# Converting 64-bit weights beside a full TensorE: squares, signs and the identity change engines

## The chip, the cores and the metric

The kernel runs on one core of a Trainium2 chip. The metric is the device time of one execution in microseconds (us). Before the change it is 718.17 us, the median of three runs (717.43 to 720.17). The engines are named as the profile names them: PE is TensorE's matmul and PEld its weight load, DVE is VectorE, ACT is ScalarE, POOL is GpSimd, SP is the queue that issues most transfers.

## The reference

The first part is attention through a small memory, for 8 batches, 8 heads, 576 tokens, head size 64 and 32 memory slots. The second part is a feed-forward layer with 512 inputs and 2048 hidden values:

```python
a = softmax(phi, axis=tokens)                # b h s m
k_m, v_m = a^T k, a^T v                      # b h m d
attn = softmax(q k_m^T / sqrt(64)) v_m       # b h s d
x = attn, heads side by side                 # 4608 x 512
h = x @ w_in
out = (h * cos(h)) @ w_out
```

The two weights `w_in` (512 x 2048) and `w_out` (2048 x 512) come as 64-bit floats; all else is float32.

## The kernel before

**Weights.** [...] Each weight is handled in eight slices of 128 partitions by 1024 numbers: `w_in` in slices of 256 columns (`load_w_in`, `convert_w_in`), `w_out` in slices of 256 rows (`load_w_out`, `convert_w_out`). Three buffers hold raw slices in turn; slices 2 and 3 of `w_in` use space of `w_out` instead. `to_float32` (lines 124 to 142) makes five steps of a slice: the sign goes to the upper half of each float32 (L133, on DVE), the last three bits of the mantissa to the lower half (L135, ACT), the high word is scaled by a power of two (L139, ACT, in place), both are joined by a shift and an or (L140, DVE), and the squares are summed along each partition (L142, ACT, which writes the squares into the raw buffer's low words).

From the sums of squares `weight_scale` (L162 to L174) gets one power of two for each weight: a maximum over the slices (L165, DVE), an all-reduce over the partitions on POOL (L166: `m_in` for `w_in`, `m_out` for `w_out`), and small DVE operations (from L167 on). The power of two brings the weight into the range of two float16 parts. `w_out_split` (L178, L179) and `w_in_split` (L189, L190) make these parts.

**Batches.** `memory(b)` makes the first softmax and `k_m`, `v_m`. For the first four batches the maximum over the tokens is a DVE reduce (L220, `nmx`) and a product with the identity on PE that puts it on all partitions (L223, `top`). It also turns `X` with the identity (L268). An all-reduce on POOL (L288, `l`) gives the batch's power of two (`v_scale`, L152 and L153). `attend(b)` makes the scores (L350) and the second softmax; `fold` multiplies `v_m` into `w_in` (L427, L433), so that one product of depth 256 takes the place of attention's last product and of the first large one.

**Large products.** The 4608 tokens are 12 groups of 384; each has 16 steps `f`, one for 128 of the 2048 hidden values. A step is `gemm1` (the first product), `act` and `act_end` (the cosine, on ACT and DVE) and, four steps later, `gemm2` (the second product). Group 0 works in float32 (L485, L533), as the scales are not known yet, and takes place while the weights arrive; the later groups work with pairs of float16 parts (L494, L538), three passes for one. Values between the two products wait in six `gp` buffers. In each step of group 0 one slice of a weight is converted (`convert_next`), in the order in0, in1 ahead of the steps, then out0, in2, in3, out1, out2, in4, in5, out3, out4, in6, in7, out5, out6, out7. After in7 `weight_scale` runs for `w_in`, after out7 for `w_out`. Group 1 needs both scales.

**Order.** A planner orders each engine's instructions ahead of time by when their inputs should be ready and by their place in the program; some are pinned behind the one before them (`keep_in_program_order`). On the chip each engine runs its list in that order. Two small PSUM banks (`small_ps`, L56) serve all small products in turn. At the start, `warm` issues idle products so that PE does not slow down.

The identity, `ident`, is made on POOL at the start (`make_identity`, a memset and an affine select, which the profile shows as masks.py:197 and masks.py:199).

Of the kernel before, what the change touches and what calls it, by code (L numbers as in the profile page):

```python
# [9 lines left out]

F16 = mybir.dt.float16
F32 = mybir.dt.float32
# [5 lines left out]
AF = mybir.ActivationFunctionType  # L18
ALU = mybir.AluOpType
# [4 lines left out]
P = 128  # L24
# [8 lines left out]
WS = 256  # L33
# [11 lines left out]
@with_exitstack  # L45
def attention_then_ffn(ctx: ExitStack, tc: tile.TileContext, phi, phiT, kv, qT, w_in, w_out, out):
    nc = tc.nc
# [11 lines left out]
    ident = const.tile([P, P], F32, name="ident")  # L59
    make_identity(nc, ident)  # L60
    # in X, heads of even number hold [k | v] and those of odd number [v | k]
    vmask = const.tile([P, 2, 2], F32, name="vmask")
# [4 lines left out]
    w_in_sb = const.tile([P, NP, DF], F32, name="w_in_sb")  # L67
    # w_out: block f + 1 holds rows f * 128 on as float32, later block f their two float16 parts
    wo = const.tile([P, NF + 1, DM], F32, name="wo")
# [30 lines left out]

# [1 line left out]
    raws = itertools.count()  # L102
# [4 lines left out]
    def load_w_in(j):  # L107
        if j in (2, 3):
            # the space of w_out's last blocks, which come later
            t = wo[:, 13:17] if j == 2 else wo[:, 9:13]  # L110
            t = t.bitcast(I32).rearrange("p c (f t) -> p c f t", t=2)
        else:
            t = ld.tile([P, NP, WS, 2], I32, tag=next_raw(), name=f"raw_in_{j}")
        nc.sync.dma_start(out=t, in_=w_in[:, 2 * WS * j:2 * WS * (j + 1)].rearrange("(c p) (f t) -> p c f t", p=P, t=2))
        loads["in", j] = t
# [7 lines left out]

    def to_float32(dst, raw, sq_to, pin=False):
        # the upper half of dst gets the sign, the lower half the last three bits of the mantissa,
        # which lead the low word. The high word as a float32 times 2^-112 has the exponent less
        # 896, three bits too low, and nothing above it.
        low, high = raw[:, :, :, 0], raw[:, :, :, 1]
        flat = raw.rearrange("p c f t -> p c (f t)")
        halves = dst.bitcast(I16).rearrange("p c (f t) -> p c f t", t=2)  # L130
        low_top = flat.bitcast(U8).rearrange("p c (f t) -> p c f t", t=8)[:, :, :, 3]
        high_top = flat.bitcast(I8).rearrange("p c (f t) -> p c f t", t=8)[:, :, :, 7]
        begin = (nc.vector.tensor_scalar(out=halves[:, :, :, 1], in0=high_top, scalar1=0.0, scalar2=-32768.0,  # L133
                                         op0=ALU.is_lt, op1=ALU.mult),
                 nc.scalar.activation(halves[:, :, :, 0], low_top, AF.Copy, scale=2.0 ** -5, bias=-31.0 / 64.0))  # L135
        if pin:
            for ins in begin:
                tc.keep_in_program_order(ins)
        nc.scalar.activation(high.bitcast(F32), high.bitcast(F32), AF.Copy, scale=2.0 ** -112)  # L139
        nc.vector.scalar_tensor_tensor(out=dst.bitcast(I32), in0=high, scalar=3, in1=dst.bitcast(I32),  # L140
                                       op0=ALU.logical_shift_left, op1=ALU.bitwise_or)
        nc.scalar.activation(low.bitcast(F32), dst, AF.Square, accum_out=sq_to)  # L142

    def convert_w_in(j):
        to_float32(w_in_sb[:, :, j * WS:(j + 1) * WS], loads.pop(("in", j)), sq[:, 0, j:j + 1], j == 1)

    def convert_w_out(j):
        to_float32(wo[:, 2 * j + 1:2 * j + 3], loads.pop(("out", j)), sq[:, 1, j:j + 1])

    # e, a power of two, with every magnitude below 2 e; and 2^14 / e  # L150
    def power_of_two(dst, src):
# [10 lines left out]
    def weight_scale(kind, name):  # L162
        # halving the exponent of the largest sum of squares
        m = const.tile([P, 1], F32, name=f"m_{name}")
        nc.vector.tensor_reduce(out=m, in_=sq[:, kind], op=ALU.max, axis=AX.X)  # L165
        nc.gpsimd.partition_all_reduce(m, m, channels=P, reduce_op=RED.max)  # L166
        nc.vector.tensor_scalar(out=m, in0=m, scalar1=2.0, scalar2=2.0 ** -100, op0=ALU.mult, op1=ALU.max)  # L167
        nc.vector.tensor_scalar(out=m.bitcast(I32), in0=m.bitcast(I32), scalar1=1, scalar2=None,
                                op0=ALU.logical_shift_right)
        nc.vector.tensor_scalar(out=m, in0=m, scalar1=2.0 ** 63, scalar2=None, op0=ALU.mult)  # L170
        e = const.tile([P, 1], F32, name=f"e_{name}")
        power_of_two(e, m)
        st["e", name] = e
        st["s", name] = to_range(f"s_{name}", const, f"s_{name}", e)  # L174
# [6 lines left out]

    # w_in in two float16 parts. A head's 64 rows of both parts are brought together on the 128
    # partitions, so that one pass takes both: the first part stays where it is, the second goes to
    # the other half. The slices are kept where a load or an earlier slice was.
    def w_in_split(q, c):
# [17 lines left out]

    # the maximum over the tokens, on all partitions, far ahead of its use
    def maximum(b):
# [7 lines left out]

# [1 line left out]
    def memory(b):  # L215
        a = loads.pop(("phi", b))
        if b < NT:
            # by the tensor engine, from phi transposed
            nmx = wk.tile([P, 2], F32, tag="nmx", name=f"nmx_{b}", bufs=1)
            nc.vector.tensor_reduce(out=nmx, in_=loads.pop(("phiT", b)), op=ALU.max, axis=AX.X)  # L220
            top = small_ps(f"top_{b}")[:, 0:HM]
            for g in range(2):
                nc.tensor.matmul(top[:, g * P:(g + 1) * P], lhsT=nmx[:, g:g + 1].broadcast_to([P, P]), rhs=ident,  # L223
                                 start=True, stop=True)
        else:
            top = st["top", b]
# [4 lines left out]
        for c0, c1, n in ((0, 2, P), (2, 4, P), (4, 5, S - 512)) if b == 0 else ((0, 4, P), (4, 5, S - 512)):  # L231
            ins = nc.vector.tensor_tensor(out=a[:n, c0:c1], in0=a[:n, c0:c1],
                                          in1=top[:n].unsqueeze(1).broadcast_to([n, c1 - c0, HM]),
                                          op=ALU.subtract)
            if b >= NT:
                # not sooner: the maximum takes its time
                tc.keep_in_program_order(ins)
            nc.scalar.activation(a[:n, c0:c1], a[:n, c0:c1], AF.Exp)  # L238
# [53 lines left out]

    # the powers of two that bring the two-part float16 operands into range
    def v_scale(b):
# [4 lines left out]
    def scales(b):  # L299
# [10 lines left out]
        else:  # L310
            # the first part of v_m for both parts of w_in, the second part for the first one alone
            sv = to_range(f"sv_{b}", wk, "sv", st["ev", b])
# [9 lines left out]

    # attention over the memory: scores with (head, memory) on the partitions; 32 by 32 blocks are
    # transposed for the softmax over a head's memory, and back
    def attend(b):
        qt, km = loads.pop(("q", b)), st["km", b]
        flat = wk.tile([P, 4 * S], F16, tag="aT", name=f"aT_{b}", bufs=3)
        # the first group works in float32, on the first GT tokens of the first batch
        t32 = GT if b == 0 else 0
# [90 lines left out]

    # v_m folded into w_in
    def fold_psum(b, q, g):
# [46 lines left out]

# [1 line left out]
    def regions(grp):  # L471
# [53 lines left out]
    def gemm2(grp, f, gp):  # L525
        if f == 0:
            # nothing else is left for the small tiles' banks beside the last group
            spare = 2 if grp == 11 else 0
# [11 lines left out]
        if f == NF - 1:  # L540
            # the last group waits for the third accumulator of the one before alone
            for t in (2,) if grp == 10 else range(3):
                evacuate(grp, t)
# [24 lines left out]

# [1 line left out]
    load_phi(0)  # L570
# [31 lines left out]
    fold_first(1)  # L602
    # the other weights, in the order in which they are needed, each a step of the first group
    todo = [("out", 0)]
# [48 lines left out]
    for i in range(12 * NF):  # L653
# [16 lines left out]
        begun.append((grp, f, hp, *act(grp, f, hp, last)))  # L670
        # with nothing else between them, a step's first half goes before the second half of the one before
        while len(begun) > (grp >= 9):
# [31 lines left out]

_INS = ["phi", "phiT", "kv", "qT", "w_in", "w_out"]

# [32 lines left out]
```

## Time and profile before

| what | value |
| --- | --- |
| median of three runs | 718.17 us |
| the profiled execution: span | 718.0 us |
| PE busy | 694.5 us |
| DVE busy | 569.6 us |
| ACT busy | 520.3 us |
| POOL busy | 14.6 us |
| mean granted clock of PE | 0.993 |
| sums of squares (L142): 16 | mean 1.16 us each, without the accumulator's read |
| signs (L133): 16 | 0.71 to 0.77 us each |
| conversions, first to last | 22 to 110 us |

The span runs from the first to the last instruction. The page of the profile gives the busy time of each engine, the chain of waits, and the costliest groups of instructions by line; the timeline lists instructions in order of time, with the idle time ahead of them and who ended it in brackets. Matmuls are pipelined and their ends are modelled, so a busy PE is not of itself one at its full pace; starts that follow each other tell more.

### The profile page before, as it was taken

How to read it: one execution, taken by the hardware profiler on the slowest of the kernel's cores; microseconds unless marked ns; L12 is line 12 of the kernel's file. 1: busy time of each engine (PE TensorE's matmuls, PEld its weight loads, DVE VectorE, ACT ScalarE, POOL GpSimd, SP SyncE). 2: the span in 40 equal slices, each digit the busy share in tenths (PEclk: the TensorE clock that was granted, in tenths of full speed). 3: DMA queues.
4: the chain of work that ended last, by engine and by line, in shares of the span. 5: the costliest groups of instructions: out<-in, count | busy, mean ns of one | idle time of the engine just before them, and what ended most of it. 6: DMA issues, size and time to landing. Idle time of an engine off the chain costs nothing.

```text
span 718.0 us, 12024 instructions
## 1 busy us (share of the span) xinstructions
PE 694.5 (97%) x4578; PEld 357.3 (50%) x4578; DVE 569.6 (79%) x1257; ACT 520.3 (72%) x964; POOL 14.6 (2%) x36
## 2 busy tenths in 40 slices
PE   6689999999999999999999999999999999999997
PEld 2345444565454444565444444566444544555553
DVE  2779999998988997589877897669776987676763
ACT  1699999889886875678756685668767785665553
POOL 0000000000000000000000100000000000000000
PEclk9799999999999999999999999999999999999999
DMA  9994981526405300152104310152100000100101
GB/s 282 382 326 159 310 306 30 132 60 188 148 8 160 110 1 1 45 166 67 45 1 135 96 48 1 45 168 67 44 1 1 22 25 1 45 1 1 45 0 45
DMA packets 31417, 66.72 MB, mean 93 GB/s; under 512 B 2176, under 2 KB 10880, under 8 KB 31360
## 3 DMA queue, kind: packets, MB, share of 16 engines
q1 hardware_dynamic: 27040, 58.09, 25.5%
q10 hardware_dynamic: 4320, 7.87, 2.9%
q8 instruction: 36, 0.59, 0.3%
q14 instruction: 21, 0.17, 0.1%
HBM read 52.31 MB, written 9.44 MB: 86 GB/s over the span
## 4 chain that ended last, share of the span: by engine, by line
PE 59%; DVE 20%; ACT 14%; issue 3%; DMA 3%; POOL 0%; SPq 0%; DVEq 0%; ACTq 0%; POOLq 0%
PE acc L538 34%; PE hp L494 18%; PE pv L433 3%; DVE u L517 3%; DVE gp L520 2%; DVE u L509 2%; DMA phi<-in_phi 2%; ACT u L513 2%; DVE gp L508 2%; ACT L513 1%; DVE vw L440 1%; PE psA L248 1%; ACT raw_out L142 1%; DVE wo L179 1%; PE sc L350 1%
## 5 line engine op out<-in xcount | busy, mean ns | idle before, releaser
L538 PE MATMUL acc<-wo,gp 128*128 128x512 f16 x1584 | 371.3, 379 | 0.0
L538 PEld LDWEIGHTS <-gp 128*128 128x128 f16 x1584 | 153.4, 98 | 161.6 <-issue 2.6
L494 PE MATMUL hp<-aT,vw 128*128 128x192 f16 (+1 forms) x1440 | 202.9, 284 | 1.4 <-DVE u L517 1.2
L494 PEld LDWEIGHTS <-vw 128*128 128x128 f16 x1440 | 125.0, 98 | 84.0 <-issue 30.7
L513 ACT ACTIVATE u<-u 128x384 f32<-128x384 f32 x192 | 99.9, 524 | 88.5 <-DVE u L509 87.4
L517 DVE SCALAR_TENSOR_TENSOR u<-hp,u 128x384 f32<-128x384 f32 x176 | 96.9, 553 | 45.8 <-ACT u L513 43.5
L503 ACT ACTIVATE u<-hp,cu 128x192 f32<-128x192 f32 (+1 forms) x240 | 110.9, 492 | 17.0 <-PE hp L494 10.8
L520 DVE TENSOR_TENSOR gp<-u,gp 128x384 f16<-128x384 f32 x176 | 96.6, 552 | 29.8 <-ACT gp L519 29.3
L519 ACT CAST gp<-u 128x384 f16<-128x384 f32 x176 | 89.2, 509 | 40.0 <-DVE u L517 37.9
L509 DVE TENSOR_TENSOR u<-u,gp 128x384 f32<-128x384 f32 x192 | 105.8, 552 | 3.1
L508 DVE CAST gp<-u 128x384 int32<-128x384 f32 x192 | 67.4, 354 | 20.4 <-ACT u L503 18.7
L533 PE MATMUL acc<-wo,gp 128*128 128x512 f32 x96 | 45.5, 599 | 0.2 <-DVE gp L515 0.2
L440 DVE SCALAR_TENSOR_TENSOR vw<-pv,vw 128x512 f16<-128x512 f32 x48 | 33.1, 689 | 4.7 <-ACT vw L439 3.4
L439 ACT ACTIVATE vw<-pv 128x512 f16<-128x512 f32 x48 | 28.3, 591 | 6.4 <-PE pv L433 5.5
L485 PE MATMUL hp<-aT,vf 128*128 128x384 f32 x64 | 26.4, 545 | 4.2 <-DVE gp L515 2.0
L513 ACT ACT_TABLE_LOAD x23 | 29.5, 1283 | 0.4
L533 PEld LDWEIGHTS acc<-wo,gp 128*128 128x128 f32 x96 | 17.2, 190 | 17.4 <-issue 12.9
L248 PE MATMUL psA<-kv,phi 128*32 128x129 f32 (+1 forms) x640 | 23.5, 277 | 0.8 <-ACT phi L238 0.8
L554 ACT ACTIVATE ob<-acc,os 128x512 f32<-128x512 f32 x28 | 18.5, 683 | 8.0 <-PE acc L538 6.1
L248 PEld LDWEIGHTS psA<-kv,phi 128*32 128x32 f32 (+1 forms) x640 | 16.0, 109 | 11.2 <-issue 5.9
L485 PEld LDWEIGHTS hp<-aT,vf 128*128 128x128 f32 x64 | 12.4, 206 | 17.2 <-issue 5.3
L350 PE MATMUL sc<-q,km 128*64 128x256 f32 (+3 forms) x192 | 20.2, 336 | 0.0
(129 smaller groups left out, 553.3 us busy)
## 6 DMA issues: line engine op xcount, KB each, us to landing
kv<-in_kv SPq DMA_DIRECT2D x32, 516.0 KB, 5.8
q<-in_qT SPq DMA_DIRECT2D x8, 1152.0 KB, 5.7
raw_out<-in_w_out SPq DMA_DIRECT2D x8, 1024.0 KB, 5.5
out<-ob ACTq DMA_DIRECT2D x30, 256.0 KB, 2.1
raw_in<-in_w_in SPq DMA_DIRECT2D x6, 1024.0 KB, 7.3
phi<-in_phi SPq DMA_DIRECT2D x8, 512.0 KB, 6.7
w_in_sb<-w_in_parts SPq DMA_DIRECT2D x12, 256.0 KB, 4.6
phiT<-in_phiT SPq DMA_DIRECT2D x4, 576.0 KB, 8.0
```

The lines of the kernel that those rows point to most:

```text
L248: nc.tensor.matmul(psA[32 * j:32 * (j + 1), g * KV:(g + 1) * KV], lhsT=a[:n, c, h * M:(h + 1) * M], rhs=kvs[c][:n, h * KV:(h + 1) * KV], s ...
L440: nc.vector.scalar_tensor_tensor(out=vw[:, 1, g], in0=src, scalar=T, in1=vw[:, 0, g], op0=ALU.mult, op1=ALU.subtract)
L494: nc.tensor.matmul(hp[:, c0:c0 + n], lhsT=vw[:, wi, g, fo * P:(fo + 1) * P], rhs=aT[:, ai, g, c1:c1 + n], start=(k == 0), stop=(k == 5))
L503: ins = nc.scalar.activation(u[:, c0:c0 + n], hp[:, c0:c0 + n], AF.Copy, scale=st["cu", b] if grp else 1.0 / (2.0 * math.pi), bias=0.25)
L508: nc.vector.tensor_copy(out=ni, in_=u)
L509: nc.vector.tensor_tensor(out=u, in0=u, in1=ni, op=ALU.subtract)
L513: nc.scalar.activation(u, u, AF.Sin, scale=TWO_PI_BELOW)
L517: nc.vector.scalar_tensor_tensor(out=u, in0=hp[:, :GT], scalar=2.0 ** -17, in1=u, op0=ALU.mult, op1=ALU.mult)
L519: nc.scalar.copy(gp[:, 0], u)
L520: nc.vector.tensor_tensor(out=gp[:, 1], in0=u, in1=gp[:, 0], op=ALU.subtract)
L533: nc.tensor.matmul(accs[grp][t], lhsT=gp[:, t * P:(t + 1) * P], rhs=wo[:, f + 1], start=(f == 0), stop=(f == NF - 1))
L538: nc.tensor.matmul(accs[grp][t], lhsT=gp[:, gi, t * P:(t + 1) * P], rhs=parts[:, wi], start=(f == 0 and gi == 0 and wi == 0), stop=(f == N ...
```

## The change

The identity becomes an input, `eye`, which the first transfer on SP's queue brings. In `to_float32` the sign's engine becomes an argument: DVE for slices 0 to 2 of `w_in`, POOL for the other five and for all eight of `w_out`. The sum of squares no longer runs on ACT. In its place PE takes the upper halves of the finished float32 numbers as bf16 (every second halfword), multiplies each of eight blocks of 128 columns with itself, and adds the eight products in one small PSUM bank; on the diagonal stand sums of squares. DVE takes the maximum of each row. The raw buffer is no longer written after L140. Where this text speaks of Gram products, it means these.

```diff
     ident = const.tile([P, P], F32, name="ident")
-    make_identity(nc, ident)
+    nc.sync.dma_start(out=ident, in_=eye)
...
-    def to_float32(dst, raw, sq_to, pin=False):
+    def to_float32(dst, raw, sq_to, by, pin=False):
...
-        begin = (nc.vector.tensor_scalar(out=halves[:, :, :, 1], in0=high_top, scalar1=0.0, scalar2=-32768.0,
-                                         op0=ALU.is_lt, op1=ALU.mult),
+        begin = (by.tensor_scalar(out=halves[:, :, :, 1], in0=high_top, scalar1=0.0, scalar2=-32768.0,
+                                  op0=ALU.is_lt, op1=ALU.mult),
...
-        nc.scalar.activation(low.bitcast(F32), dst, AF.Square, accum_out=sq_to)
+        tops = dst.bitcast(BF16).rearrange("p c (f t) -> p c f t", t=2)
+        gram = small_ps("gram")[:, 0:P]
+        cols = [tops[:, c, x:x + P, 1] for c in range(dst.shape[1]) for x in range(0, dst.shape[2], P)]
+        for i, w in enumerate(cols):
+            nc.tensor.matmul(gram, lhsT=w, rhs=w, start=(i == 0), stop=(i == len(cols) - 1))
+        nc.vector.tensor_reduce(out=sq_to, in_=gram, op=ALU.max, axis=AX.X)
 
     def convert_w_in(j):
-        to_float32(w_in_sb[:, :, j * WS:(j + 1) * WS], loads.pop(("in", j)), sq[:, 0, j:j + 1], j == 1)
+        to_float32(w_in_sb[:, :, j * WS:(j + 1) * WS], loads.pop(("in", j)), sq[:, 0, j:j + 1],
+                   nc.vector if j < 3 else nc.gpsimd, j == 1)
 
     def convert_w_out(j):
-        to_float32(wo[:, 2 * j + 1:2 * j + 3], loads.pop(("out", j)), sq[:, 1, j:j + 1])
+        to_float32(wo[:, 2 * j + 1:2 * j + 3], loads.pop(("out", j)), sq[:, 1, j:j + 1], nc.gpsimd)
```

More of the change, by code (lines that the diff above doesn't have):

```diff
@@ L7 @@
 from concourse import bass_isa, mybir
-from concourse.masks import make_identity
 from concourse._compat import with_exitstack
+BF16 = mybir.dt.bfloat16
 F16 = mybir.dt.float16
@@ L45, in attention_then_ffn @@
 @with_exitstack
-def attention_then_ffn(ctx: ExitStack, tc: tile.TileContext, phi, phiT, kv, qT, w_in, w_out, out):
+def attention_then_ffn(ctx: ExitStack, tc: tile.TileContext, phi, phiT, kv, qT, w_in, w_out, eye, out):
     nc = tc.nc
@@ L702, in attention_then_ffn @@
         gemm2(*p)
-_INS = ["phi", "phiT", "kv", "qT", "w_in", "w_out"]
+_INS = ["phi", "phiT", "kv", "qT", "w_in", "w_out", "eye"]
 def kernel(**inputs):
@@ L725 @@
         "w_out": np.ascontiguousarray(w_out).view(np.int64),
+        "eye": np.eye(P, dtype=np.float32),
     }
```

## The prediction

> **What bounds the kernel now.** I read the page's span first, then the busy time by stage, then the timeline of PE, then the start and GpSimd's queue.
>
> ```profile
> span 718.0 us, 12024 instructions
> ```
>
> ```profile
> 0.00:46.00 46.00, 30.13 (x180) 14.38 (x182) 23.86 (x49) 22.63 (x29) 1.84 (x10) 0.89 0.99 331
> 46.00:112.00 66.00, 65.47 (x308) 31.36 (x305) 62.86 (x136) 65.78 (x100) 1.94 (x6) 1.00 0.72 249
> ```
>
> The second fence gives, for a stage, the busy time of PE, PEld, DVE, ACT and POOL, then the granted clock, the DMA share and GB/s. The profiled execution took 718.0 us and the median of the three times is 718.17, so I sum against 718. All conversions of weights lie before 112 us. From 46 to 112 us PE, DVE and ACT are all busy 95% or more, and a busy PE need not be a full one. The timeline of PE settles it:
>
> ```profile
> 61.85 0.61 PE L268 MATMUL tpx<-ident,X 128*128 128x128 f32 x4
> 62.30 1.02 PE L533 MATMUL acc<-wo,gp 128*128 128x512 f32 x2
> 63.16 0.49 PE L485 MATMUL hp<-aT,vf 128*128 128x384 f32 x1
> ```
>
> Two float32 passes of 512 columns give way to the next after 0.86 us (63.16 less 62.30), four of 128 after 0.45 us: 0.84 and 0.88 ns a column. Long and short ones run at one pace, so it is the columns that take the time and no pauses hide in the busy share. After 46 us, then, two things alone change the time: work that PE gains or loses, and inputs so late that PE stops. Before 46 us PE idles for 15.9 us, and a faster start pays one for one.
>
> **Start: the identity by DMA.** First from the chain of waits, then the timeline, then the DMA issues with their us to landing:
>
> ```profile
> 0.87 0.32 POOL km L271
> ...
> 1.24 0.01 POOLq masks.py:199
> 1.25 9.56 issue
> ```
>
> ```profile
> 4.65 1.35 DVE L220 TENSOR_REDUCE nmx<-phiT 128x2 f32<-128x1152 f32 x1 [2.96 <-DMA phiT<-in_phiT]
> 5.12 0.59 SPq L98 DMA_DIRECT2D q<-in_qT  x1
> 6.05 3.90 SPq L114 DMA_DIRECT2D raw_in<-in_w_in  x2
> 11.14 1.22 PE L223 MATMUL top<-ident,nmx 128*128 128x128 f32 x4 [4.94 <-POOL ident masks.py:199]
> 22.08 1.37 ACT L135 ACTIVATE w_in_sb<-raw_in 128x1024 int16<-128x1024 uint8 x1
> 22.42 1.52 PE L350 MATMUL sc<-q,km 128*64 128x256 f32 x16
> 26.27 1.12 ACT L139 ACTIVATE raw_in<-raw_in 128x1024 f32<-128x1024 f32 x1 [2.81 <-DVE w_in_sb L133]
> 27.42 1.23 DVE L140 SCALAR_TENSOR_TENSOR w_in_sb<-raw_in,w_in_sb 128x1024 int32<-128x1024 int32 x1 [0.36 <-ACT raw_in L139]
> ```
>
> ```profile
> q<-in_qT SPq DMA_DIRECT2D x1, 1152.0 KB, 13.2
> raw_in<-in_w_in SPq DMA_DIRECT2D x1, 1024.0 KB, 15.0
> ```
>
> The first maximum `top` has its `nmx` at 6.0 and starts at 11.14, for the identity. One more issue at the head of SP's queue pushes the others by some 0.5 us (an issue's own time), so `top` could start at 6.5, 4.6 us sooner. Other inputs end most of this. The batch's q lands at 18.3 (5.12 + 13.2); after the same push the scores can start 3.6 us sooner than 22.42. The first raw slice lands at 21.05 (6.05 + 15.0), and the chain L135, L139, L140 of 3.72 us then ends at 25.3 and not at 28.65, 3.4 us sooner. I take 3.1, between bounds of 0.5 (what L135 itself can move) and 4.6.
>
> **ScalarE loses the squares.** A row of the groups by line, and two of the waits:
>
> ```profile
> L142 ACT ACTIVATE raw_out<-wo 128x1024 f32<-128x1024 f32 x8 | 9.3, 1165 | 0.1
> ```
>
> ```profile
> PE hp L485 <- DVE gp L515: 2.0, 1, 2.0
> ...
> PE hp L485 <- ACT vf L458: 0.7, 1, 0.7
> ```
>
> Sixteen times 1.165 us is 18.6 us of ACT. After 46 us that is no gain by itself, as PE is full. Before, it is worth what PE waits for in its first steps behind ACT's queue, 2.0 + 0.7 us. I take 2.0, bounds 0 and 2.7. The raw buffers also come free a square earlier, so SP can issue the next raw loads sooner.
>
> **TensorE gains the Gram products:** eight matmuls of 128 by 128 bf16 for each of 16 slices, each with its own weight load. No row has this form. The float32 passes above give 0.112 us for 128 columns (0.45 by four), an upper bound. The timeline gives a lower one; the groups by line have what VectorE needs:
>
> ```profile
> 114.81 1.15 PE L494 MATMUL hp<-aT,vw 128*128 128x192 f16 x12
> 115.81 1.05 PE L533 MATMUL acc<-wo,gp 128*128 128x512 f32 x2
> ```
>
> ```profile
> L133 DVE TENSOR_SCALAR wo<-raw_out 128x1024 int16<-128x1024 int8 x8 | 6.0, 755 | 0.0
> ...
> L282 DVE TENSOR_REDUCE l<-X 128x4 f32<-128x256 f32 x2 | 0.8, 411 | 0.0
> ```
>
> Twelve f16 products of 192 columns give way after 1.00 us, 83 ns each, with a weight load of the same size hidden; by columns, 128 would be 56 ns. I take 70, between that and the 83, which is the nearest row. Thirteen of the 16 slices fall into the full stretch: 104 x 70 ns = 7.3 us, bounds 5.8 and 11.6. The other three fall into idle time. Their banks come from the two small ones and are freed by VectorE's maximum. That reduce is some 0.25 us (half the elements of the row of 0.41): 16 x 0.25 = 4.0 us more for DVE, against 13 signs less, 13 x 0.755 = 9.8. DVE gains 5.8 us, which the full PE hides.
>
> If nothing else happened: 718.0 - 3.1 - 2.0 + 7.3 = 720.2.
>
> **GpSimd gains 13 signs.** This decides. From GpSimd's timeline:
>
> ```profile
> 0.73 0.20 POOL masks.py:197 MEMSET ident<- 128x128 f32 x1 [0.29 <-POOLq L727]
> ...
> 10.80 0.28 POOL masks.py:199 TENSOR_SCALAR_AFFINE_SELECT ident<-ident 128x128 f32<-128x128 f32 x1 [9.62 <-issue]
> ...
> 21.40 0.38 POOL L288 PARTITION_ALL_REDUCE l<-l  x1 [9.79 <-DVE l L286]
> ...
> 66.59 0.37 POOL L288 PARTITION_ALL_REDUCE l<-l  x1 [19.37 <-DVE l L286]
> ...
> 96.09 0.35 POOL L166 PARTITION_ALL_REDUCE m_in<-m_in  x1 [18.32 <-DVE m_in L165]
> ...
> 110.42 0.35 POOL L166 PARTITION_ALL_REDUCE m_out<-m_out  x1 [13.73 <-DVE m_out L165]
> ...
> 231.56 1.09 POOL L211 PARTITION_ALL_REDUCE mx<-mx  x1 [4.31 <-DVE mx L210]
> ```
>
> The price of one: memsets of 128 and 256 elements take 0.20 and 0.32 us, 0.9 ns an element more, so 0.95 us for 1024 is the lower end. The affine select's 0.28 for 128 would make 2.3 us, the all-reduce's 1.09 for 256 would make 4.4. The sign is a comparison and a multiplication on bytes eight apart, into halfwords four apart; I take 4.4, nearest to the all-reduce as work of several steps for each element.
>
> The affine select stood 9.56 us behind a mark of the queue, with nothing shown that released it. Memsets have no such gap, and the first all-reduce comes after 9.8 idle us, in which one could hide. I read the gap as code being fetched for another kind of instruction. The sign is another kind than the all-reduce, and the new queue mixes them: the all-reduces of l_0 and l_1 (line 288), m_in and m_out (line 166) lie among the signs. I take 9.56 us for each change of kind.
>
> The Trainium skill, GPSIMD Engine Reference, section 2.1, has such libraries of loadable code, and gives the first call after a load some 6 us. The 9.56 us here agree in kind and are longer; by its figure each change below would cost 3.6 us less.
>
> The queue, worked out on the old times: l_0 comes at 18, the first change ends at 28, and seven signs (out0, in3, out1, out2, in4, in5, out3) fit before l_1, which I put at 65 (66.6 less 5.1 from the start, and six slices' products more). Then two changes and the all-reduce, 65 + 19.1 + 0.4 = 84.5. The signs of out4, in6 and in7 last until 97.7. Now m_in could start at 100.4 (L140, products and reduces: 2.7), but out5's sign runs until 102.1; with its change m_in starts at 111.7 and not 96.1. Change back, 121.6; out6 and out7 until 130.4; their tail of 2.7 and the last change: m_out at 142.7, not 110.4.
>
> ```profile
> 114.85 0.75 DVE L179 SCALAR_TENSOR_TENSOR wo<-wo,s_out 128x512 f16<-128x512 f32 x1
> ...
> 127.10 0.81 PE L538 MATMUL acc<-wo,gp 128*128 128x512 f16 x3
> ```
>
> From m_out to the first split block of w_out are 5.2 us (110.42 to 115.60), so the first f16 product, now at 127.1, comes at 147.9, 20.8 us later. Meanwhile PE can go one step of first products ahead (six `gp` buffers, five in use): the 1.00 us of above. The Gram products and the start's gain then lie inside PE's wait. All engines execute in order: behind L152 and L167, which wait for an all-reduce, stands the rest of DVE's work, and behind a Gram product of a late slice all of PE's. **Forecast: 718.0 + 20.8 - 1.0 = 737.8, say 738.** Bounds: with signs at 0.95 us the same queue has m_out before 125, which hides it all, and leaves the 720 of above. If the earlier stops, at out4's slice and at m_in, are not made good, each may add what a change costs, some 10 us.
>
> **Rivals.**
>
> *GpSimd locks VectorE.* From the timeline of both:
>
> ```profile
> 562.07 0.56 DVE L520 TENSOR_TENSOR gp<-u,gp 128x384 f16<-128x384 f32 x1
> 562.19 0.65 POOL L288 PARTITION_ALL_REDUCE l<-l  x1 [69.40 <-DVE l L286]
> ```
>
> This all-reduce takes 0.65 us, not 0.35, beside a DVE operation with two operands in SBUF, and ends after it. If DVE in turn waits for whole signs, then 11 signs after 46 us at half of 4.4 us each are 24 us, on a DVE with 3.1 idle and 5.8 freed: 15 us on top, 753. Against it: no row has DVE waiting. Chance 0.15. The Trainium skill, SBUF — State Buffer, section on SBUF's two separate sides, has an exclusive lock in both directions; the row agrees for the one.
>
> *No change of kind is paid*, or an order hides it. Then the sum above holds, 720.2. Thirteen signs of 4.4 us are 57 of the 84 us from 28 to 112. For it: one gap alone is seen for sure. Chance 0.16.
>
> *Faster: the start decides.* GpSimd keeps up as in the last, and the full stretch begins much sooner: by 4.6 from the identity, 2.7 from the squares, and 2.3 because the first steps of group 0 no longer run at a slow pace after an idle PE:
>
> ```profile
> 32.20 5.46 PE L485 MATMUL hp<-aT,vf 128*128 128x384 f32 x8 [1.43 <-DVE aT L373]
> ...
> 43.24 1.56 PE L485 MATMUL hp<-aT,vf 128*128 128x384 f32 x4 [1.98 <-DVE gp L515]
> ```
>
> Eight took 5.46 us, and twice four later ones would take 3.12. With products at 56 ns: 718.0 - 9.6 + 5.8 = 714.2. It is faster from 9.4 us gained at the start on. Against it: DMA is busy 0.99 of that stage, and sets when the slices come. Chance 0.13.
>
> **How the numbers follow.** Forecast 0.56, lock 0.15, nothing paid 0.16, faster 0.13. A measurement can tell about 0.5% here, 3.6 us. Faster: 0.13. Same: the most of the 720 case and the lower edge of the forecast, 0.17. Slower: 0.70. The range reaches from 713, under the faster case, to 762, the lock with part of the 10 us; the forecast's own range is 722 to 750.
>
> **What would show it.** Right: gaps near 9.6 us on POOL before all-reduces and before signs that follow them, signs near 4.4 us, m_out near 143, and over 15 us of idle PE between 75 and 150 us. The start is right if `top` begins near 6.5 and the first L485 near 29. Wrong: POOL without such gaps, or PE full from 46 us on; then the time is near 720, or less if the full stretch begins by 37.

## The result, and the profile after

The changed kernel takes 758.37 us (median of four runs, 756.71 to 760.93), against 718.75 for the kernel before on the same chip: a ratio of 1.0541 [1.0509, 1.0572]. It is slower by twice what was forecast. The profiled execution took 757.45 us. Line numbers of the changed kernel are 7 or 8 higher from `weight_scale` on: the first product of group 0 is L493 (L485 before), that of the later groups L502 (L494), the second products L541 and L546 (L533 and L538).

The page of the changed kernel, its span, its busy times and its clock:

```profile
span 755.6 us, 12282 instructions
...
PE 709.2 (94%) x4706; PEld 368.8 (49%) x4706; DVE 573.0 (76%) x1259; ACT 507.0 (67%) x933; POOL 68.6 (9%) x47
...
PEclk9679899799999999999999999999999999999999
```

Busy time by stage, the kernel before and then the changed one (PE, PEld, DVE, ACT, POOL, granted clock, DMA share, GB/s; the first two stages of the kernel before stand in the prediction):

```profile
112.00:170.00 58.00, 57.26 (x365) 31.77 (x363) 57.83 (x118) 53.36 (x110) 0.31 (x1) 1.00 0.33 79
```

```profile
0.00:46.00 46.00, 23.35 (x158) 11.25 (x158) 21.70 (x44) 16.30 (x18) 10.34 (x10) 0.76 0.91 319
46.00:112.00 66.00, 55.98 (x340) 30.32 (x340) 48.63 (x95) 47.74 (x62) 34.19 (x11) 0.91 0.71 242
112.00:170.00 58.00, 49.68 (x201) 24.18 (x200) 39.67 (x96) 36.12 (x63) 13.23 (x6) 0.90 0.16 51
```

All is lost before 170 us. In those 170 us PE is busy for 129.01 us instead of 152.86, and a part of that at half clock; what follows is 585.6 us of span instead of 548.0. The 46 us at the start, where the forecast saw a gain, lose 6.8 us of PE's work.

GpSimd's timeline in the changed kernel (start, duration, instruction, idle time ahead and what ended it):

```profile
17.30 0.35 POOL L296 PARTITION_ALL_REDUCE l<-l  x1 [15.76 <-DVE l L294]
26.72 4.04 POOL L133 TENSOR_SCALAR wo<-raw_out 128x1024 int16<-128x1024 int8 x1 [9.07 <-DMA raw_out<-in_w_out]
32.12 4.94 POOL L133 TENSOR_SCALAR w_in_sb<-wo 128x1024 int16<-128x1024 int8 x1 [1.36 <-DMA wo<-in_w_in]
52.33 0.31 POOL L279 MEMSET km<- 128x256 f32 x1 [15.27 <-PE sc L358]
52.61 7.98 POOL L133 TENSOR_SCALAR wo<-raw_out 128x1024 int16<-128x1024 int8 x2
...
87.53 0.43 POOL L296 PARTITION_ALL_REDUCE l<-l  x1 [5.96 <-issue]
97.51 4.05 POOL L133 TENSOR_SCALAR wo<-raw_out 128x1024 int16<-128x1024 int8 x1 [9.55 <-ACT u L511]
...
116.10 0.38 POOL L174 PARTITION_ALL_REDUCE m_in<-m_in  x1 [6.29 <-issue]
...
123.47 11.84 POOL L133 TENSOR_SCALAR wo<-raw_out 128x1024 int16<-128x1024 int8 x3 [6.74 <-issue]
143.91 0.76 POOL L174 PARTITION_ALL_REDUCE m_out<-m_out  x1 [8.60 <-DVE m_out L173]
```

A sign takes 4.0 to 5.1 us, and before each change between signs and all-reduces GpSimd stands still for 6 to 9.6 us. `m_out` comes at 143.9; the forecast had 142.7. One idle stretch was not foreseen: the memset of `km` at 52.33 waits 15.27 us for the scores of batch 0 on PE, and two signs stand behind it.

PE at the start of the changed kernel:

```profile
16.76 0.61 PE L276 MATMUL tpx<-ident,X 128*128 128x128 f32 x4
24.97 1.03 PE L148 MATMUL gram<-w_in_sb 128*128 128x128 bf16 x8 [7.61 <-DVE w_in_sb L140]
25.81 2.33 PE L590 MATMUL warm<-zeros 128*128 128x512 f16 x5
28.07 2.83 PE L358 MATMUL sc<-q,km 128*64 128x256 f32 x16
43.29 2.90 PE L493 MATMUL hp<-aT,vf 128*128 128x384 f32 x4 [11.25 <-DVE aT L381]
```

The Gram products of the first slice stand ahead of the scores in PE's order. They wait 7.61 us for the slice, and the scores wait with them. The first product of group 0 comes at 43.29, not near 29.

PE at the end of the conversions, from the timeline and from the windows of the changed kernel:

```profile
129.94 1.03 PE L148 MATMUL gram<-wo 128*128 128x128 bf16 x8 [4.35 <-DVE wo L140]
...
137.95 1.01 PE L148 MATMUL gram<-wo 128*128 128x128 bf16 x8 [3.97 <-DVE sq L149]
...
144.21 1.98 PE L541 MATMUL acc<-wo,gp 128*128 128x512 f32 x4
...
...
168.61 1.67 PE L546 MATMUL acc<-wo,gp 128*128 128x512 f16 x7
```

```profile
120.00:142.00 22.00, 13.68 (x43) 6.20 (x42) 8.52 (x14) 11.36 (x17) 11.84 (x3) 0.80 0.00 0
142.00:170.00 28.00, 28.00 (x130) 13.90 (x128) 26.14 (x58) 21.21 (x41) 0.76 (x1) 0.97 0.23 66
```

The first f16 second product comes at 168.61, 24.7 us after `m_out` and not 5.2. PE isn't waiting for the split in those 24.7 us: it is full from 142 us on, with float32 products of group 0 that it could not do while the slices were late. The first split block of `w_out` is ready at 150.59 us (L187, at 149.85 for 0.74 us), 18 us before PE comes to it.

### The profile page after: what moved, and what is told of

Same layout as the page of the kernel before. It is cut to its first block, busy times and chain, and to the rows that moved or that the text cites. A ratio compares the mean times of both kernels' runs of the same rounds, so it can differ in the third digit from the quotient of the medians.

```text
span 755.6 us, 12282 instructions
## 1 busy us (share of the span) xinstructions
PE 709.2 (94%) x4706; PEld 368.8 (49%) x4706; DVE 573.0 (76%) x1259; ACT 507.0 (67%) x933; POOL 68.6 (9%) x47
## 4 chain that ended last, share of the span: by engine, by line
PE 66%; DVE 13%; ACT 7%; POOL 5%; DMA 4%; issue 3%; SPq 1%; ACTq 0%; POOLq 0%; DVEq 0%
PE acc L546 37%; PE hp L502 19%; POOL wo L133 4%; PE pv L441 3%; DMA raw_out<-in_w_out 3%; DVE u L517 2%; PE psA L256 2%; DMA phi<-in_phi 2%; DVE u L525 1%; PE sc L358 1%; DVE gp L528 1%; DVE gp L516 1%; DVE wo L187 1%; POOL w_in_sb L133 1%; DVE vw L448 1%
## 5 line engine op out<-in xcount | busy, mean ns | idle before, releaser
L546 PE MATMUL acc<-wo,gp 128*128 128x512 f16 x1584 | 370.7, 379 | 0.0
L546 PEld LDWEIGHTS <-gp 128*128 128x128 f16 x1584 | 153.6, 98 | 161.3 <-issue 1.8
L502 PE MATMUL hp<-aT,vw 128*128 128x192 f16 (+1 forms) x1440 | 202.1, 284 | 0.4 <-DVE u L525 0.3
L502 PEld LDWEIGHTS <-vw 128*128 128x128 f16 x1440 | 125.0, 98 | 80.7 <-issue 28.0
L511 ACT ACTIVATE u<-hp,cu 128x192 f32<-128x192 f32 (+1 forms) x240 | 110.5, 490 | 19.9 <-PE hp L502 14.0
L517 DVE TENSOR_TENSOR u<-u,gp 128x384 f32<-128x384 f32 x192 | 108.3, 565 | 3.4
L541 PE MATMUL acc<-wo,gp 128*128 128x512 f32 x96 | 48.3, 630 | 0.0
L493 PE MATMUL hp<-aT,vf 128*128 128x384 f32 x64 | 28.8, 573 | 13.6 <-DVE aT L381 11.2
L133 POOL TENSOR_SCALAR wo<-raw_out 128x1024 int16<-128x1024 int8 x8 | 33.0, 4146 | 32.0 <-DMA raw_out<-in_w_out 15.7
L296 POOL PARTITION_ALL_REDUCE l<-l x8 | 4.0, 504 | 333.5 <-DVE l L294 327.6
L541 PEld LDWEIGHTS acc<-wo,gp 128*128 128x128 f32 x96 | 18.2, 199 | 18.2 <-issue 15.4
L493 PEld LDWEIGHTS hp<-aT,vf 128*128 128x128 f32 x64 | 13.1, 220 | 26.3 <-issue 18.5
```

The lines of the kernel that those rows point to most:

```text
L133: begin = (by.tensor_scalar(out=halves[:, :, :, 1], in0=high_top, scalar1=0.0, scalar2=-32768.0, op0=ALU.is_lt, op1=ALU.mult), nc.scalar.a ...
L493: nc.tensor.matmul(hp[:, :GT], lhsT=st["vf", q][:, g, fo * P:(fo + 1) * P], rhs=st["aTf"][:, g], start=(g == 0), stop=(g == 1))
L502: nc.tensor.matmul(hp[:, c0:c0 + n], lhsT=vw[:, wi, g, fo * P:(fo + 1) * P], rhs=aT[:, ai, g, c1:c1 + n], start=(k == 0), stop=(k == 5))
L511: ins = nc.scalar.activation(u[:, c0:c0 + n], hp[:, c0:c0 + n], AF.Copy, scale=st["cu", b] if grp else 1.0 / (2.0 * math.pi), bias=0.25)
L517: nc.vector.tensor_tensor(out=u, in0=u, in1=ni, op=ALU.subtract)
L541: nc.tensor.matmul(accs[grp][t], lhsT=gp[:, t * P:(t + 1) * P], rhs=wo[:, f + 1], start=(f == 0), stop=(f == NF - 1))
```

## The experiments

The theory after the result: two losses of nearly equal size. GpSimd's queue delays the slices by about the forecast's term, and beside it the first slice's Gram products hold up PE's queue at the start, which the forecast had at nothing. The rivals: the lock between GpSimd and VectorE; the length of the signs alone; the Gram products' own work. To compare kernels timed beside different runs of the kernel before, "+x us" below is (ratio − 1) times 720 us, about the median of the kernel before throughout. The changed kernel is then +39.0.

**One part undone.** All signs back on VectorE, the rest of the change as it is:

```diff
-                   nc.vector if j < 3 else nc.gpsimd, j == 1)
+                   nc.vector, j == 1)
...
-        to_float32(wo[:, 2 * j + 1:2 * j + 3], loads.pop(("out", j)), sq[:, 1, j:j + 1], nc.gpsimd)
+        to_float32(wo[:, 2 * j + 1:2 * j + 3], loads.pop(("out", j)), sq[:, 1, j:j + 1], nc.vector)
```

> The changed kernel, but all 16 signs stay on VectorE. Queue theory (GpSimd's signs and its changes of kind make the slices and both scales late): most of the loss goes, 715 to 727 us, with Gram products and the identity's transfer still in. Gram theory (the products on PE, their work and their place in PE's order, make the loss): 745 us or more. Start theory (the loss is made before 46 us by the new order at the start): the first product of group 0 (L493) still near 43 us, and the time near 729.

Measured: 730.63 us, 1.0148 [1.0117, 1.0178], +10.7. The windows of this kernel:

```profile
0.00:46.00 46.00, 23.04 (x168) 11.36 (x170) 23.47 (x48) 16.58 (x19) 1.36 (x8) 0.81 0.93 320
46.00:112.00 66.00, 65.53 (x396) 34.90 (x393) 60.79 (x139) 60.14 (x80) 2.60 (x5) 1.00 0.75 258
```

Without signs on GpSimd, PE is full from 46 us on, as before the change. So the signs make all the stops after 46 us, 28 us of the loss. But the start stays as slow as in the changed kernel (23.04 us of PE's work, 23.35 there, 30.13 before; the first product at 41.63 us): GpSimd's signs have no part in that. This is what the start theory expected: a late first product, and a time near 729.

The squares back on ScalarE, the rest as it is:

```diff
-        tops = dst.bitcast(BF16).rearrange("p c (f t) -> p c f t", t=2)
...
-        nc.vector.tensor_reduce(out=sq_to, in_=gram, op=ALU.max, axis=AX.X)
+        nc.scalar.activation(low.bitcast(F32), dst, AF.Square, accum_out=sq_to)
```

> The changed kernel, but the squares are summed on ScalarE again; signs on GpSimd and the identity's transfer stay. Queue theory: the changes of kind stay, m_out stays near 140 us, and the time is 735 to 755. Gram theory: 722 us or less. If PE is held mainly because Gram products of late slices stand ahead of other work in its order, the time lies between, near 735.

Measured: 737.65 us, 1.0256 [1.0229, 1.0284], +18.4. From its PE timeline, and from its GpSimd timeline:

```profile
18.77 1.52 PE L353 MATMUL sc<-q,km 128*64 128x256 f32 x16
...
28.56 4.43 PE L488 MATMUL hp<-aT,vf 128*128 128x384 f32 x8 [1.43 <-DVE aT L376]
...
74.10 1.98 PE L459 MATMUL pvf<-w_in_sb,vm 128*64 128x256 f32 x8 [4.62 <-DVE w_in_sb L140]
...
82.50 1.98 PE L459 MATMUL pvf<-w_in_sb,vm 128*64 128x256 f32 x8 [4.72 <-DVE vf L461]
...
143.12 0.81 PE L541 MATMUL acc<-wo,gp 128*128 128x512 f16 x3 [0.76 <-ACT ob L553]
```

```profile
59.38 1.26 POOL L291 PARTITION_ALL_REDUCE l<-l  x1 [5.99 <-issue]
67.52 7.92 POOL L133 TENSOR_SCALAR w_in_sb<-raw_in 128x1024 int16<-128x1024 int8 x2 [6.88 <-issue]
...
135.23 0.38 POOL L169 PARTITION_ALL_REDUCE m_out<-m_out  x1 [5.89 <-DVE u L512]
```

The start is now as forecast: scores at 18.77, first product at 28.56. What is left is GpSimd's queue, and it alone costs what the forecast gave for the whole. But PE does not stand still where the forecast put it, behind `m_out`. It idles for 4.8 us from 46 to 75 us and for 8.6 us from 75 to 120 us (where the granted clock is 0.84). The two longest stops are shown: 4.62 us for a slice of `w_in` whose sign came at 67.52, behind the all-reduce `l` and two changes of kind, and 4.72 us for a copy, `vf`, that stands behind two more late slices in VectorE's order. From 120 to 143 us PE idles for 1.1 us. The first split block of `w_out` is ready at 141.84 us, and PE is busy with earlier products until 142.35. The stops at and after 143.12, 3.0 us in all, end with group 0's results being copied out (`ob`), in part by a VectorE that is busy for 8.9 of the 9 us from 143 to 152.

It follows that the sums of squares on TensorE cost 20.6 us in the changed kernel.

**One part alone.** The kernel before with the identity by DMA, and nothing else of the change:

```diff
-    make_identity(nc, ident)
+    nc.sync.dma_start(out=ident, in_=eye)
```

> The kernel before, with nothing changed but the identity, which comes by DMA. By the prediction's term the start gains 3.1 us: 715. Start theory (the earlier identity makes the planner choose a worse order on PE and VectorE): slower, up to 729.

Measured: 720.09 us over ten runs, 1.0002 [0.9989, 1.0015], +0.1. The first product starts 1.2 us sooner (30.98), but the product with the first slice waits longer (`pvf L456`, 5.8 us in the waits, 5.1 before) and later stops give the rest back (`acc L533` waits 1.6 us for VectorE, 0.2 before).

The kernel before with the Gram block in place of the square:

```diff
-        nc.scalar.activation(low.bitcast(F32), dst, AF.Square, accum_out=sq_to)
+        tops = dst.bitcast(BF16).rearrange("p c (f t) -> p c f t", t=2)
...
+            nc.tensor.matmul(gram, lhsT=w, rhs=w, start=(i == 0), stop=(i == len(cols) - 1))
+        nc.vector.tensor_reduce(out=sq_to, in_=gram, op=ALU.max, axis=AX.X)
```

> The kernel before, with nothing changed but the squares, which become Gram products on PE. By the prediction's terms 7.3 us more on PE and 2.0 less at the start: 723. Gram theory: 740 or more. If ScalarE's relief were worth more than the products cost: under 716.

Measured: 733.72 us, 1.0197 [1.0175, 1.0219], +14.2. Its PE timeline:

```profile
26.44 1.03 PE L147 MATMUL gram<-w_in_sb 128*128 128x128 bf16 x8 [4.45 <-DVE w_in_sb L141]
27.28 2.33 PE L588 MATMUL warm<-zeros 128*128 128x512 f16 x5
29.54 2.73 PE L356 MATMUL sc<-q,km 128*64 128x256 f32 x16
...
43.96 2.26 PE L491 MATMUL hp<-aT,vf 128*128 128x384 f32 x3 [10.45 <-DVE aT L379]
```

The time lies between the readings. The picture is that of the changed kernel, without any sign on GpSimd: products, warm products, scores, and the first product of group 0 at 43.96.

The kernel before with 13 signs on GpSimd, the identity still made there (the diff is the one of the change, for `by` alone):

```diff
-        begin = (nc.vector.tensor_scalar(out=halves[:, :, :, 1], in0=high_top, scalar1=0.0, scalar2=-32768.0,
+        begin = (by.tensor_scalar(out=halves[:, :, :, 1], in0=high_top, scalar1=0.0, scalar2=-32768.0,
```

> The kernel before, with nothing changed but the 13 signs, which go to GpSimd; the identity is made there too, so one more change of kind comes at the start. Queue theory: slower by 15 to 45 us, 735 to 760, with gaps of 6 to 10 us at each change of kind. Gram theory: within 5 us of before.

Measured: 740.86 us, 1.0289 [1.0261, 1.0318], +20.8. Here `m_out` comes at 140.52 and the first f16 second product at 148.44, 7.9 us after it, as with the squares on ScalarE (135.23 and 143.12). Again PE does not wait for `m_out`: it idles for 12.2 us from 75 to 120 us and for 0.6 us from 120 to 143 us.

**What makes up the signs' price.** The changed kernel with the four early all-reduces (`l_0`, `l_1`, `m_in`, `m_out`) replaced by a product with the identity and a maximum, so that GpSimd runs nothing but signs and memsets while weights arrive:

```diff
+    def all_max(dst, src, name):
+        t = small_ps(name)[:, 0:P]
+        nc.tensor.matmul(t, lhsT=src.broadcast_to([P, P]), rhs=ident, start=True, stop=True)
+        nc.vector.tensor_reduce(out=dst, in_=t, op=ALU.max, axis=AX.X)
...
-        nc.gpsimd.partition_all_reduce(m, m, channels=P, reduce_op=RED.max)
+        all_max(m, m, f"all_{name}")
```

> The changed kernel, but the four small all-reduces of the first stage (l_0, l_1, m_in, m_out) are made by a product with the identity on PE and a maximum on VectorE, so that no change of kind lies among the signs, which stay on GpSimd. If the changes of kind make the loss: 718 to 730 us, with signs back to back. If the length of the signs (4 us and not 0.75) makes it: 740 or more.

Measured: 743.63 us, 1.0332 [1.0308, 1.0355], +23.9. Some of GpSimd's timeline:

```profile
52.92 8.00 POOL L133 TENSOR_SCALAR wo<-raw_out 128x1024 int16<-128x1024 int8 x2
...
76.65 9.48 POOL L133 TENSOR_SCALAR wo<-raw_out 128x1024 int16<-128x1024 int8 x2 [7.27 <-DMA raw_out<-in_w_out]
...
111.41 5.07 POOL L133 TENSOR_SCALAR wo<-raw_out 128x1024 int16<-128x1024 int8 x1 [1.01 <-DMA raw_out<-in_w_out]
```

With one kind of instruction left, no sign has an idle gap ahead of it that nothing ends: each waits for a transfer or not at all. The last sign ends at 116.5 instead of 135.3. The changes of kind thus cost 15.1 us of the 39.0 in this kernel. Most of the loss stays, as the second reading has it; beside the signs' length the Gram products are still in it.

The changed kernel with the sign of `w_out`'s first slice on VectorE:

```diff
-        to_float32(wo[:, 2 * j + 1:2 * j + 3], loads.pop(("out", j)), sq[:, 1, j:j + 1], nc.gpsimd)
+        to_float32(wo[:, 2 * j + 1:2 * j + 3], loads.pop(("out", j)), sq[:, 1, j:j + 1], nc.gpsimd if j else nc.vector)
```

> The changed kernel, but the sign of w_out's first slice stays on VectorE. If VectorE's wait for this one sign (behind which the first softmax stands in its order) makes the late start: the first product of group 0 (L493) comes near 36 us and not at 43, and the time falls by 5 to 8 us. If the Gram products of the first slice, which stand ahead of the scores in PE's order, make it: L493 moves by 2 us at most.

Measured: 759.29 us over three executions (a fourth, of 3223 us, is left out, and with it the only trace), 1.0533 [1.0489, 1.0577], +38.4. The time is that of the changed kernel, so this sign on GpSimd is not what costs it. Where the first product of group 0 starts here is not on record.

The kernel before with the identity by DMA and the maxima on PE, so that no change of kind stands in GpSimd's queue while weights arrive (the two diffs above together):

> The kernel before, with the identity by DMA and the four small all-reduces of the first stage made on PE and VectorE; nothing else changed. No code is fetched by GpSimd ahead of 180 us. If GpSimd's part in the start is only the identity: as with the identity alone, within 2 us. A candidate for a kernel better than both: 713 or less.

Measured: 717.49 us over ten runs, 0.9971 [0.9948, 0.9995], −2.1. Measured again:

> The same kernel as e8, in five rounds, since its gain was at the edge: 0.3% faster than before, interval below 1. If the start's 2.7 us are given back to inputs that come later: no more than 2 us faster.

Measured: 718.5 us over twelve runs, 0.9985 [0.9969, 1.0001], −1.1. At most 0.3% faster than the kernel before, and not certainly that: beside the identity alone, which makes no difference, it is the only version here that is not slower.

**Where the Gram products stand.** The changed kernel, with the first slice's Gram products issued after the scores and the first fold; nothing else of the program is changed, though the planner then orders every engine anew:

```diff
+        if later:
+            st["late"] = dst, sq_to
+            return
+        squares(dst, sq_to)
...
+    squares(*st.pop("late"))
```

> The changed kernel, but the Gram products of w_in's first slice are issued behind the scores and the first fold and not ahead of them. If their place in PE's order makes the late start: the scores start near 19 us and not at 28, the first product of group 0 (L499 here) near 30 and not at 43, and the time falls by 5 to 6 us, to about 752. If VectorE's order makes it (rival): L499 stays after 40.

Measured: 745.09 us, 1.0357 [1.0337, 1.0378], +25.7. Its PE timeline:

```profile
18.55 1.52 PE L364 MATMUL sc<-q,km 128*64 128x256 f32 x16
25.36 1.98 PE L470 MATMUL pvf<-w_in_sb,vm 128*64 128x256 f32 x8 [5.29 <-DVE w_in_sb L140]
27.27 1.03 PE L154 MATMUL gram<-w_in_sb 128*128 128x128 bf16 x8
28.76 5.33 PE L499 MATMUL hp<-aT,vf 128*128 128x384 f32 x8 [0.46 <-DVE aT L387]
```

Eight matmuls in another place make the kernel 13.3 us faster. That is over twice what I expected, and not all of it is their place on PE: GpSimd's second all-reduce `l` now comes at 59.80 us and not at 87.53, ahead of three signs that it stood behind. The same move in the kernel before with the Gram products:

> The kernel before with Gram products alone (733.7), those of the first slice again behind the scores. Place theory: the start is that of the kernel before, and what is left of the loss is PE's own work, 6.5 us: 725 to 728. Rival (the products cost more than their streaming throughout): 731 or more.

Measured: 721.98 us, 1.0038 [1.0021, 1.0055], +2.7, where the Gram block without the move had +14.2. I had expected 725 to 728. So the place costs 11.5 us of the 14.2, here without signs on GpSimd. What is left, the products' work less ScalarE's relief, is 2.7.

Last, the signs on GpSimd with none of the rest in their way: identity by DMA, squares on ScalarE, maxima on PE (diffs above):

> Signs on GpSimd and the identity by DMA, squares on ScalarE, the four small all-reduces on PE and VectorE: no change of kind among the signs and no Gram products. If the parts add (changes of kind 15, Gram products 14 to 21): 722 to 726. If the signs' length alone still stops PE as long as in e6: 735 or more.

Measured: 725.2 us, 1.0084 [1.0062, 1.0106], +6.0, within the 722 to 726 of the first reading. That is 8.1 us more than the same kernel without the signs (−2.1; 7.1 by its second measurement): what signs on GpSimd cost by their length and their place in its queue, without any change of kind.

## Why the prediction was wrong

The sign of the result was right, and so was GpSimd's queue as one cause, with about its size. The size of the whole was 20 us short, for a term that stood at nothing. And the wait of PE that the forecast put behind `m_out` lies elsewhere.

**GpSimd's queue: right in cause, near in size.** The forecast's 20.8 us less 1.0 stand against +18.4 (signs with the start in order) and +20.8 (signs alone). A sign was put at 4.4 us and took 4.0 to 5.1. A change of kind was put at 9.56 and took between 5.96 and 9.55; the Trainium skill, GPSIMD Engine Reference, section 2.1, gives some 6 us, which the shorter gaps agree with and the longer ones don't. `m_in` was put at 111.7 and came at 116.1, `m_out` at 142.7 and 143.9. Part of that agreement is luck: the second `l` came at 87.53 and not at 65, out5's sign came after `m_in` and not before it, the changes were shorter, and the wait behind the memset of `km` was not in the sum. That the changes are paid at all is shown by replacing the all-reduces (+39.0 to +23.9), so the rival "no change of kind is paid" falls. That code is fetched in these gaps stays a reading: the trace shows idle time alone.

**The step that failed** is "The other three fall into idle time", with its sequel "The Gram products and the start's gain then lie inside PE's wait". The three early slices' products were priced by their length, and their place in PE's order wasn't asked for. All the Gram products together cost 20.6 us in the changed kernel (+39.0 against +18.4), 13.3 of them by the place of the first slice's. There the first slice's products stand behind `tpx` and ahead of five warm products and the scores. The scores' inputs are there from about 18.4 us on (with the products moved, the scores run at 18.55), but they start at 28.07: 7.61 us of waiting for the slice, 0.84 for the products, 2.3 for the warm ones. Two things make 9.5 us into 14.5 at the first product of group 0 (43.29 against 28.76). The scores run at half clock after the wait (granted 0.50 from 24.97 to 30.90 us), 2.83 us and not 1.52. And the first softmax on VectorE and ScalarE now meets the conversions of the next slices. VectorE's timeline in the changed kernel, from the scores on:

```profile
30.09 1.30 DVE L360 STREAM_TRANSPOSE at<-sc 128x512 f32<-128x512 f32 x2 [3.76 <-PE sc L358]
31.97 1.23 DVE L140 SCALAR_TENSOR_TENSOR wo<-raw_out,wo 128x1024 int32<-128x1024 int32 x1 [0.57 <-ACT raw_out L139]
...
34.66 0.94 DVE L365 TENSOR_TENSOR at<-at,rm 128x768 f32<-128x768 f32 x1
35.95 1.22 DVE L140 SCALAR_TENSOR_TENSOR w_in_sb<-wo,w_in_sb 128x1024 int32<-128x1024 int32 x1 [0.35 <-ACT wo L139]
...
40.05 1.22 DVE L140 SCALAR_TENSOR_TENSOR w_in_sb<-wo,w_in_sb 128x1024 int32<-128x1024 int32 x1 [0.34 <-ACT wo L139]
41.20 0.95 DVE L375 TENSOR_TENSOR at<-at,rs 128x768 f32<-128x768 f32 x1
42.18 1.16 DVE L381 STREAM_TRANSPOSE aT<-at 128x256 f32<-128x256 f32 x4
```

Three L140 of some 1.22 us lie between `at` and `aT`; from the scores' start to the first product are 15.2 us here and 10.2 with the products moved.

The later slices' products do it too. PE idles for 15.5 us from 75 to 150 us in the changed kernel, as the prediction's signs had it, but all of this stands ahead of Gram products of late slices, 4.35 and 3.97 us of it in the rows at 129.94 and 137.95. With the squares on ScalarE it idles for 12.0 us there. From 120 to 143 us it is 8.3 us against 1.1.

**The start's gain: its first part right, its effect wrong.** `top` started at 6.41 (forecast 6.5), and the first slice's L140 ended at 24.9 (25.3). With the squares on ScalarE the first product came at 28.56 (29). But 1.2 us at the start gained by the identity alone were worth nothing in the time, +0.1 us. So "a faster start pays one for one" did not hold. My reading is that the later slices' transfers set the pace there, as the DMA share is 0.99 until 46 us in the kernel before; no run took that apart.

**The wait at `m_out`: wrong too.** The prediction has "the first f16 product, now at 127.1, comes at 147.9, 20.8 us later", as if PE had run out of float32 work when the scale is known. In the kernel before, PE is full for the 16.7 us between the two. In the kernels with signs on GpSimd, too, no wait of PE ends with the split: the late slices stop it earlier, in group 0, and what they held up is still to be done when `m_out` comes. That takes 7.9 us in both kernels with the squares on ScalarE, 18.7 with the first products moved (137.35 to 156.01), and 24.7 in the changed one. The prediction named these earlier stops, but as something that might come on top. That its 20.8 lies near +18.4 and +20.8 is luck as far as the place of the stop goes.

The two losses make each other worse. The kernel with all signs on VectorE keeps +10.7 and the one with the squares on ScalarE +18.4, together 10 us less than +39.0. The trace shows how they meet: the late scores hold up the memset of `km`, and so the signs behind it (52.33 us; 42.93 with the squares on ScalarE), and the signs make the slices late for which the Gram products wait. How much of the 10 us each makes is not shown.

**The Gram products' own work** was put at 7.3 us, 5.3 with ScalarE's relief of 2.0 taken off. It is +2.7 in the time where the slices are on time and the first slice's products stand behind the scores. With signs on GpSimd, where the slices are late, it is 7.3 (+25.7 with the first ones moved, +18.4 with none). At full clock one was put at 70 ns and took 58 to 80 (last section). VectorE's maximum took 0.282 us and not 0.25 (groups by line of the changed kernel, 0 to 170 us):

```profile
L148 PE MATMUL gram<-w_in_sb 128*128 128x128 bf16 x64 | 6.3, 253 | 14.2 <-DVE w_in_sb L140 10.2 <-ACT vf L466 4.0
...
L149 DVE TENSOR_REDUCE sq<-gram 128x1 f32<-128x128 f32 x16 | 4.5, 282 | 5.8 <-PE gram L148 5.6
```

The 14.2 us are idle time of PE ahead of the products of `w_in`'s eight slices: half of it is the one wait at the start.

**The faster case** needed 9.4 us gained at the start, and PE's first 46 us lost 6.8 us of work instead. **The lock: not seen at its price.** From 32.12 to 37.06 us GpSimd runs a sign. In it lie L365 (0.94 us) and L140 at 35.95 (1.22 us), both with two operands in SBUF, and both as long as in the kernel before (0.94 and 1.23). The sign is the one that grows, to 4.94 us. The Trainium skill, SBUF — State Buffer, section on SBUF's two separate sides, has such an operation wait for the whole of the other engine's instruction; these rows don't show it. Some operations do take longer beside a sign: L517, never over 0.56 us after 170 us, took 1.28, 1.35 and 1.39 us at 77.83, 97.71 and 66.02. That is 0.7 to 0.8 us more, not a sign's 4.

**The sum.** The runs make one line from the changed kernel to the one before, one step at a time: the first Gram products moved (39.0 to 25.7), then the squares on ScalarE (18.4), then the maxima on PE (6.0), then the signs on VectorE (−2.1), then the identity and the maxima back on GpSimd (0). So +39.0 is 13.3 for the place of eight matmuls, 7.3 for the Gram products otherwise, 12.4 for changes of kind, 8.1 for the signs without them, and −2.1 for identity and maxima. The steps have these sizes in this order only: taken first, the changes of kind are 15.1. The planner also orders each kernel anew, which no run takes apart.

## What to carry to other kernels

When a step moves to an engine that works in a fixed order, ask first where in that order it will stand and when its input arrives, and only then how long it is: eight matmuls of under a microsecond in all cost 11 to 13 us ahead of the scores. All 128 cost 3 us where their slices came in time, and 7 where the slices were late. On GpSimd count the changes between kinds of instruction, at 6 to 10 us each here, as carefully as the instructions. Before a late scale goes into a sum, ask whether the engine will have run out of other work when it comes: here the late slices had stopped PE before. And two delays need not hide each other: what cost 10.7 and 18.4 us alone cost 39.0 together.

## What was not expected of the hardware

The changes of kind on GpSimd are not one price. In the changed kernel they left 5.96, 9.55, 6.29 and 6.74 us of idle time that no input ends (for the 9.55 the view names L511, which writes nothing that a sign reads). Over this kernel, the one with the squares on ScalarE, the one with signs alone and the one with the first products moved, there is a pattern, if gaps that an input ends are left out. A change to an all-reduce took 5.7 to 6.4 us, eleven times. A change to a sign took 6.7 to 7.4 us with DMA idle (a share of 0.01 or less), four times. With a DMA share of 0.93 or more it took 9.1 to 9.6 us three times, but 6.88 and 7.48 us the other two. What decides stays open. That the code comes by the queues that the weights use would fit in part; no run tried it.

The price of a Gram product depends on what ran before it. After the wait of 7.61 us, eight of them gave way to the next after 0.84 us (25.81 less 24.97), 105 ns each. In full work it is half that or a little more. PE's timeline of the changed kernel:

```profile
53.29 0.62 PE L148 MATMUL gram<-w_in_sb 128*128 128x128 bf16 x8
53.75 2.80 PE L493 MATMUL hp<-aT,vf 128*128 128x384 f32 x8
```

That is 0.46 us for eight, 58 ns each; ahead of a fold (L464) eight gave way after 0.55 us (49.88 to 50.43), 69 ns each, and once after 0.64 us (112.72 to 113.36), 80 ns each. The Trainium skill, TensorE: Matmul & The Clock Gate, part 1, has 106.7 and 55.6 ns for 128 columns at the two clocks, and half clock after an idle window of some 3.4 us; 105 and 58 ns agree with the two, and the 7.61 us ahead of the slow ones with the window.
